# Pooled attention and MLP mixer on one core: u transposed in pairs, a second v buffer, and the fourth batch's loads in another order

## The chip, the core and the metric

The kernel runs on one core of a Trainium2 chip. The metric is the device time of one execution in microseconds; lower is better. Before the change it is 290.57 us, the median of 3 runs from 289.85 to 290.57.

## What is computed

Eight batches, each with q, k, v of 8 heads x 576 positions x 64. Keys and values are averaged over groups of 8 positions (576 become 72), softmax attention runs over the 72, and the result x (576 x 512 per batch) goes through a token-mixing and a channel-mixing MLP, each with its residual:

```
k_p, v_p = mean over groups of 8 positions of k, v          # 72 x 64 per head
x  = softmax(q k_p^T / 8) v_p                               # heads side by side: 576 x 512
u  = x + (relu(x^T w_tok1) w_tok2)^T                        # 576 -> 256 -> 576 along positions
out = u + relu(u w_ch1) w_ch2                               # 512 -> 1536 -> 512 along channels
```

Inputs and output are float32; the kernel computes in bfloat16 and sums in float32.

## The kernel before

A batch's 576 positions are cut into 4 chunks of 128 (main) and a tail of 64; the tails of two batches share one tile of 128 (pairs 0 and 7, 1 and 2, 3 and 4, 5 and 6). Below, "second batch" is `b` = 1, "fourth batch" is `b` = 3, and so on.

One batch passes these steps. Loads by GpSimd's queue, which cast to bfloat16 on the way (`load`: k into `km`, q into `qm`, v into `vs`, tails into `kt` and `qt`). q transposed by DMA on SyncE's queue (`qT_dma`, L540; for the first two batches by TensorE). k pooled by matmuls (`pool_k`); v pooled by matmuls for the first two batches (`pool_v`, L288) and by adds on GpSimd for the others (`sum_v`, L298 to L300). Scores of two units of half the main positions each (`a` and `c` in the code; the first and the second unit) and a tail unit (`do_S`, L326, with the row maximum and the subtraction on VectorE, L329 and L331), the exponential on ScalarE (`do_E`, L339), the probabilities transposed by DMA from SyncE's queue (`do_PT`, L346, two for a unit; for the first two batches by TensorE), and their product with v (`do_AV`, L387). Token mixing (`do_AT`, L472; `do_u`, L510, its sum with x on VectorE, L515). Then u is transposed (`do_uT`, L526: by DMA for all but the first batch, one transfer for each chunk of 128 positions into `uTm`, laid out as 4 blocks of channels x 512 positions). Channel mixing reads it (`channel_mix`): L756 multiplies `w_ch1` with a whole row of 512 positions, so it needs all four chunks; ScalarE applies the ReLU into `GT` (L758); L771 multiplies `GT` with `w_ch2`, chunk by chunk, VectorE adds u (L775), and the output goes out by SyncE's queue (L803).

The order of work is written out. `weave` mixes two lists of steps by their estimated costs: the channel mixing of batch b as the main list, and beside it the value products and token mixing of batch b + 1 and the scores of batch b + 2. Every engine takes its instructions strictly in that order, and so does each queue: SyncE issues transposes and outputs one after the other, and GpSimd both issues the loads and does the sums of v. A step of cost 0 is put in without moving the others.

The loads of the first four batches are issued ahead, as far as buffers allow; those of batch b + 2 from the fifth on wait for a gate: GpSimd copies one column of the second unit's last transposed probabilities (L739) and then issues the loads.

```
def load_gated(b, ready):
    nc.gpsimd.tensor_copy(out=gate, in_=ready())
    load(b, (0, 2, 1) if slot_of[b] else (0, 1, 2))      # 0 is k, 1 is q, 2 is v
    sum_v(b)
```

k and q have two buffers, v has one, so that the fourth batch's v is loaded after the third's is summed, from the list of the second batch (L670, L671). `GT` has two buffers. PSUM gives six buffers to all the matmuls' results. At most eight loads of GpSimd's queue are in flight: the next one waits for the landing of the one eight before it; the same holds for SyncE's queue.

Of the kernel before, what the change touches and what calls it, by code (L numbers as in the profile page):

```python
# [9 lines left out]
BF16 = mybir.dt.bfloat16  # L10
# [5 lines left out]
class Stream:  # L16
# [5 lines left out]
    def add(self, cost, fn):  # L22
        self.items.append((cost, fn))
# [25 lines left out]
def kernel(  # L49
# [16 lines left out]
    nc = tc.nc  # L66
# [15 lines left out]

    singles = ctx.enter_context(tc.tile_pool(name="singles", bufs=1))
    kv_pool = ctx.enter_context(tc.tile_pool(name="kv", bufs=2))
    v_pool = ctx.enter_context(tc.tile_pool(name="vp", bufs=1))
    sum_pool = ctx.enter_context(tc.tile_pool(name="sums", bufs=1))
    tail_pool = ctx.enter_context(tc.tile_pool(name="tl", bufs=2))
    pt_pool = ctx.enter_context(tc.tile_pool(name="ptp", bufs=6))
# [4 lines left out]
    u_pool = ctx.enter_context(tc.tile_pool(name="up", bufs=2))  # L93
    at_pool = ctx.enter_context(tc.tile_pool(name="atp", bufs=3))
    ut_pool = ctx.enter_context(tc.tile_pool(name="utail", bufs=2))
    gt_pool = ctx.enter_context(tc.tile_pool(name="gt", bufs=2))
    out_pool = ctx.enter_context(tc.tile_pool(name="outp", bufs=4))
    ps = ctx.enter_context(tc.tile_pool(name="ps", bufs=6, space=bass.MemoryType.PSUM))
    ps_tr = ctx.enter_context(tc.tile_pool(name="ps_tr", bufs=2, space=bass.MemoryType.PSUM))
# [15 lines left out]

    def load(b, which=(0, 1, 2)):
        g = group_of[b]
        if (b == 2 or g > 1 and slot_of[b] == 0) and 0 in which:
            tail_t[b] = [tail_pool.tile([P, H, D], BF16, name=n) for n in ("kt", "qt")]
            if b == 2:  # L120
                for t in tail_t[b]:
                    nc.gpsimd.memset(t[half[0]], 0.0)
            else:
                tail_t[groups[g][1]] = tail_t[b]
        main_t.setdefault(b, [None] * 3)
        for i in which:
            src = (k, q, v)[i]
            if i == 2 and b > 1:

                vs = v_pool.tile([P, H, POOL, D], BF16, name="vs")  # L130
                nc.gpsimd.dma_start(out=vs[0:SP].rearrange("p h t d -> p h (t d)"),
                                    in_=src[b].rearrange("h (p t) d -> p h (t d)", t=POOL))
                main_t[b][i] = vs
                continue
            mt = (v_pool.tile([P, H, POOL, D], BF16, name="vs")[:, :, 0:NJ, :] if i == 2 else
                  kv_pool.tile([P, H, NJ, D], BF16, name=("km", "qm")[i]))
            main_t[b][i], tt = mt, tail_t[b][i]
            nc.gpsimd.dma_start(out=mt.rearrange("p h j d -> p h (j d)"),
                                in_=src[b, :, 0:MAIN, :].rearrange("h (p j) d -> p h (j d)", j=NJ))

            for bb in [b] if g < 2 else groups[g] if slot_of[b] == 0 else []:
                nc.gpsimd.dma_start(out=tt[half[slot_of[bb]]], in_=src[bb, :, MAIN:S, :].rearrange("h p d -> p h d"))
# [316 lines left out]
    def token_mix(b):  # L459

        g, s = group_of[b], slot_of[b]
        ATs[b] = singles.tile([P, 2, DM], BF16, name="AT0") if b == 0 else at_pool.tile([P, 2, DM], BF16, name="AT")

        def acts(m, at_ps):
            if m == 0:
                nc.scalar.activation(out=ATs[b][:, m, :], in_=at_ps, func=AF.Relu)  # L466
            else:
                nc.vector.tensor_scalar(out=ATs[b][:, m, :], in0=at_ps, scalar1=0.0, scalar2=None, op0=ALU.max)  # L468

        def mains(m, at_ps):  # L470
            for j in range(NJ):
                nc.tensor.matmul(out=at_ps, lhsT=w1m[:, j, m * P:(m + 1) * P], rhs=x_main[b][:, j, :],  # L472
                                 start=(j == 0), stop=False)

        def tails(m, at_ps):
            nc.tensor.matmul(out=at_ps, lhsT=w1t[s][:, m * P:(m + 1) * P], rhs=x_tail[g], start=False, stop=True)  # L476

        def do_AT(m):
            at_ps = ps.tile([P, DM], FP32, name="pa")
            mains(m, at_ps)  # L480
            tails(m, at_ps)
            acts(m, at_ps)

        at_both = []

        def do_both_AT(js, tail, last):

            fresh = not at_both
            if fresh:
                at_both.extend(ps.tile([P, DM], FP32, name="pa") for _ in range(2))  # L490
            for i, j in enumerate(js):
                for m in range(2):
                    nc.tensor.matmul(out=at_both[m], lhsT=w1m[:, j, m * P:(m + 1) * P], rhs=x_main[b][:, j, :],
                                     start=(fresh and i == 0), stop=(last and i == len(js) - 1))
            if tail:
                for m in range(2):
                    nc.tensor.matmul(out=at_both[m], lhsT=w1t[s][:, m * P:(m + 1) * P], rhs=x_tail[g],
                                     start=False, stop=False)
            if last:
                for m in range(2):  # L500
                    acts(m, at_both[m])

        def do_u(j):
            u_ps = ps.tile([P, DM], FP32, name="pa")
            by_act = b == 0 and j % 2 == 1
            if j < NJ:
                if by_act:
                    nc.tensor.matmul(out=u_ps, lhsT=ident, rhs=x_main[b][:, j, :], start=True, stop=False)
                for m in range(2):
                    nc.tensor.matmul(out=u_ps, lhsT=w2m[:, m, j, :], rhs=ATs[b][:, m, :],  # L510
                                     start=(m == 0 and not by_act), stop=(m == 1))
                if by_act:
                    nc.scalar.copy(out=u_main[b][:, j, :], in_=u_ps)
                else:
                    nc.vector.tensor_tensor(out=u_main[b][:, j, :], in0=u_ps, in1=x_main[b][:, j, :], op=ALU.add)  # L515
            else:
                for i in range(4):
                    nc.tensor.matmul(out=u_ps, lhsT=w2t[i // 2][:, i % 2, :], rhs=ATs[groups[g][i // 2]][:, i % 2, :],  # L518
                                     start=(i == 0), stop=(i == 3))
                nc.vector.tensor_tensor(out=u_tail[g], in0=u_ps, in1=x_tail[g], op=ALU.add)  # L520

        def do_uT(j):
            us = u_main[b][:, j, :] if j < NJ else u_tail[g]
            if b > 0:
                dst = uT_main[b][:, :, j * P:(j + 1) * P] if j < NJ else uT_tail[g]
                nc.sync.dma_start_transpose(out=dst, in_=us)  # L526
                return
            uT_ps = ps_tr.tile([P, 4, P], BF16, name="pt")
            for kk in range(4):
                nc.tensor.transpose(out=uT_ps[:, kk, :], in_=us[:, kk * P:(kk + 1) * P], identity=ident)  # L530
            copy = nc.scalar.copy if j % 2 else nc.vector.tensor_copy
            copy(out=uT_main[b][:, :, j * P:(j + 1) * P], in_=uT_ps)

        return do_AT, do_both_AT, do_u, do_uT

# [31 lines left out]
    def mix_stream(st, b, pooled=()):  # L567
# [1 line left out]
        g, s = group_of[b], slot_of[b]  # L569
        add = adder(st)  # L570
        u_main[b] = u_pool.tile([P, NJ, DM], BF16, name="um")
        uT_main[b] = u_pool.tile([P, 4, MAIN], BF16, name="uTm")
        if s == 1:
            u_tail[g] = ut_pool.tile([P, DM], BF16, name="ut")
            uT_tail[g] = ut_pool.tile([P, 4, P], BF16, name="uTt")
# [4 lines left out]
        add(1080, do_AT, 1)  # L580
        for bb in pooled:
            add(KP, pool_k, bb)
        nj = NJ + s
        for j in range(nj + 1):
            if j < nj:
                add(690, do_u, j)
            if j >= 1:
                add(0 if b else 224, do_uT, j - 1)

    def first_stream():  # L590

# [53 lines left out]
    def second_stream(st):  # L645
# [21 lines left out]
        add(AV, a.do_AV, 0)  # L667
        add(SC, c.do_S, 2)
        add(0, t.do_E)
        add(0, load, 3, (2,))  # L670
        add(0, sum_v, 3)  # L671
        add(AV, a.do_AV, 1)
        add(0, c.do_E, 2)
        add(PT, t.do_PT)
# [62 lines left out]
    def load_gated(b, ready):  # L737

        nc.gpsimd.tensor_copy(out=gate, in_=ready())  # L739
        load(b, (0, 2, 1) if slot_of[b] else (0, 1, 2))  # L740
        sum_v(b)

    def channel_mix(uTs, us, dst, width, early=0):
# [6 lines left out]
        def do_GT(m0):  # L750
            def f():
                g_ps = ps.tile([P, per, width], FP32, name="pa")
                for i in range(per):
                    m = m0 + i
                    for kk in range(4):
                        nc.tensor.matmul(out=g_ps[:, i, :], lhsT=wc1[:, kk, m * P:(m + 1) * P], rhs=uTs[:, kk, :],  # L756
                                         start=(kk == 0), stop=(kk == 3))
                nc.scalar.activation(out=GT[:, m0:m0 + per, :], in_=g_ps, func=AF.Relu)  # L758
            return f
# [22 lines left out]
        def do_early(m, hold, t0, t1):  # L782
            def f():
                if t0 == 0:
                    hold[m] = ps.tile([P, width], FP32, name="pa")
                for kk in range(4):
                    nc.tensor.matmul(out=hold[m][:, t0:t1], lhsT=wc1[:, kk, m * P:(m + 1) * P], rhs=uTs[:, kk, t0:t1],
                                     start=(kk == 0), stop=(kk == 3))
                if t1 == width:
                    nc.scalar.activation(out=GT[:, m, :], in_=hold[m], func=AF.Relu)  # L790
# [6 lines left out]
    def c_stream(b):  # L797
# [8 lines left out]
            for s, bb in enumerate(groups[g]):  # L806
                nc.sync.dma_start(out=out[bb, MAIN:S, :], in_=o_sb[half[s], :])

        wide, chunk = channel_mix(uT_main[b], lambda j: u_main[b][:, j, :], dst_main, MAIN, 0 if b else 3)
        blocks = [wide] + [chunk(j, 2 if b == B - 1 and j == NJ - 1 else 1) for j in range(NJ)]  # L810
        if slot_of[b] == 1:
            wide, chunk = channel_mix(uT_tail[g], lambda j: u_tail[g], dst_tail, P)
            at = 3 if b == B - 1 else len(blocks)
            blocks[at:at] = [wide, chunk(0)]
        for block in blocks:
# [7 lines left out]
    load(1)  # L823
    load_w_ch2()
    load(2)
    load(3, (0, 1))
    sum_v(2)
    engines = {mybir.EngineType.PE, mybir.EngineType.Activation, mybir.EngineType.DVE,
               mybir.EngineType.SP, mybir.EngineType.Pool}
# [42 lines left out]
```

## Time and profile before

| | |
|---|---|
| median of 3 runs | 290.57 us (289.85 to 290.57) |
| profiled execution, first to last instruction (span) | 288.5 us |
| TensorE busy | 271.0 us (94%) |
| VectorE / ScalarE / GpSimd busy | 162.4 / 121.3 / 101.5 us |
| mean granted TensorE clock | 0.994 |
| moved by DMA | 42.68 MB, 148 GB/s |

A run's time has about 2 us beside the span. In the profile PE is TensorE's matmul, PEld its weight load, DVE VectorE, ACT ScalarE, POOL GpSimd and SP SyncE; a q behind a name is the engine's sequencer, which waits and issues DMAs. A row of a timeline gives the start, the duration, the engine, the line, the operation, the tiles (out<-in), shapes, the number of instructions merged, and in brackets how long the engine had been idle and what ended that. Rows for a tile or line give the shortest, median and longest duration in ns, and the time from a DMA's issue to its landing. Consecutive rows of PE overlap by some 0.2 us, since matmuls are pipelined.

### The profile page before, as it was taken

The page shows a single profiled execution, that of the slowest core. Times are in us where ns is not written, and L with a number is a line of the kernel's source. Part 1 is how long each engine was busy: PE and PEld are TensorE (multiplying, and loading weights), DVE is VectorE, ACT ScalarE, POOL GpSimd, SP SyncE. Part 2 cuts the span into 40 slices and gives each one's busy share as a digit, 9 for nine tenths or more (in the row PEclk, how much of TensorE's full clock was granted, in tenths as well). Part 3 has the DMA queues.
Part 4 walks back from the last instruction along what each step waited for, and adds up shares of the span by engine and source line. Part 5 has one row for each costly group of instructions (what it writes and reads, how often), then busy time and mean ns, then how long its engine had stood idle before and what let it go on. Part 6 is the DMA issues. An engine that isn't in the chain of part 4 may idle for free.

```text
span 288.5 us, 5632 instructions
## 1 busy us (share of the span) xinstructions
PE 271.0 (94%) x2210; PEld 147.1 (51%) x2246; DVE 162.4 (56%) x371; ACT 121.3 (42%) x222; POOL 101.5 (35%) x147
## 2 busy tenths in 40 slices
PE   6888998885999999999999999999999999999995
PEld 4554755442445554446545554465445444464463
DVE  4676268687356985386647953684558642530012
ACT  8572887113442355114553365035442561026320
POOL 8666634292780836129508423570000000000000
PEclk9999999999899999999999999999999999999999
DMA  7999999999959999998999799959524820241013
GB/s 84 185 205 198 196 204 192 174 203 146 252 88 169 166 214 195 182 183 166 172 185 155 170 218 153 157 165 162 115 54 97 194 58 36 93 109 39 27 45 110
DMA packets 102714, 42.68 MB, mean 148 GB/s; under 512 B 72480, under 2 KB 98080, under 8 KB 102688
## 3 DMA queue, kind: packets, MB, share of 16 engines
q0 software_dynamic: 36688, 17.93, 47.2%
q1 hardware_dynamic: 65856, 24.26, 43.7%
q8 instruction: 17, 0.28, 0.4%
q10 hardware_dynamic: 144, 0.13, 0.1%
q14 instruction: 9, 0.07, 0.1%
HBM read 35.85 MB, written 9.44 MB: 157 GB/s over the span
## 4 chain that ended last, share of the span: by engine, by line
PE 82%; DMA 7%; DVE 6%; ACT 3%; issue 1%; DVEq 0%
PE pa L756 31%; PE pa L771 28%; DMA qT<-qm 4%; PE pa L510 4%; PE pa L472 4%; PE pa L387 3%; DMA uTm<-um 3%; PE pa L253 2%; PE pa L326 2%; DVE sh L331 2%; DVE mx L329 1%; PE pa L267 1%; ACT prob_m L339 1%; PE pa L518 1%; ACT pT L352 1%
## 5 line engine op out<-in xcount | busy, mean ns | idle before, releaser
L771 PE MATMUL pa<-wc,GT 128*128 128x512 bf16 (+1 forms) x429 | 102.7, 373 | 1.0 <-DVE sh L331 0.2
L756 PE MATMUL pa<-uTm,wc 128*128 128x512 bf16 x357 | 90.1, 384 | 3.8 <-DMA uTm<-um 3.1
L758 ACT ACTIVATE GT<-pa 128x512 bf16<-128x512 f32 x105 | 62.5, 597 | 66.5 <-PE pa L756 62.4
L756 PEld LDWEIGHTS <-wc 128*128 128x128 bf16 x564 | 45.4, 98 | 40.6 <-DVE o L775 3.6
L771 PEld LDWEIGHTS <-GT 128*128 128x128 bf16 x444 | 41.5, 98 | 40.4
L339 ACT ACTIVATE prob_m<-sh 128x432 bf16<-128x432 f32 (+1 forms) x48 | 24.7, 522 | 60.9 <-DVE sh L331 51.1
L298 POOL TENSOR_TENSOR s<-vs 72x512 f32<-72x512 bf16 x24 | 27.6, 1148 | 49.7 <-DMA vs<-in_v_dram 48.2
L775 DVE TENSOR_TENSOR o<-pa,um 128x512 f32<-128x512 f32 (+1 forms) x33 | 22.1, 670 | 25.3 <-PE pa L771 25.3
L329 DVE TENSOR_REDUCE mx<-pa 128x6 f32<-128x432 f32 (+1 forms) x48 | 26.4, 550 | 7.6 <-PE pa L326 7.5
L331 DVE TENSOR_TENSOR sh<-pa,mx 128x432 f32<-128x432 f32 (+1 forms) x48 | 26.8, 558 | 5.1 <-DVE mx L329 0.5
L391 DVE RECIPROCAL den<-pa 128x4 f32<-128x4 f32 (+1 forms) x66 | 11.6, 176 | 24.5 <-PE pa L387 24.4
L515 DVE TENSOR_TENSOR um<-pa,xm 128x512 bf16<-128x512 f32 x30 | 20.2, 687 | 8.6 <-PE pa L510 8.6
L392 DVE TENSOR_TENSOR xm<-pa,den 128x256 bf16<-128x256 f32 x56 | 23.8, 424 | 1.9
L510 PE MATMUL pa<-AT,w2m 128*128 128x512 bf16 x64 | 18.3, 379 | 0.5 <-ACT AT L466 0.5
L299 POOL TENSOR_TENSOR s<-s 72x256 f32<-72x256 f32 x24 | 17.3, 722 | 1.9
L468 DVE TENSOR_SCALAR AT<-pa 128x512 bf16<-128x512 f32 x8 | 5.5, 692 | 21.8 <-PE pa L476 21.1
L387 PEld LDWEIGHTS <-pT 72*128 72x128 bf16 (+1 forms) x280 | 12.4, 100 | 8.8 <-issue 1.7
L326 PE MATMUL pa<-kbd,qT 128*128 128x144 bf16 x128 | 15.5, 226 | 1.4 <-DMA qT<-qm 0.9
L326 PEld LDWEIGHTS <-qT 128*128 128x128 bf16 x128 | 10.7, 98 | 10.5 <-DMA qT<-qm 1.4
L387 PE MATMUL pa<-vpx,pT 72*128 72x65 bf16 (+1 forms) x280 | 14.1, 194 | 1.1 <-DVE pT L352 0.5
L472 PE MATMUL pa<-xm,w1m 128*128 128x512 bf16 x54 | 14.4, 379 | 0.4 <-DVE xm L392 0.2
L253 PE MATMUL pa<-idle 128*128 128x288 bf16 (+2 forms) x40 | 9.8, 379 | 2.3 <-DVE pool_t L178 2.2
(122 smaller groups left out, 232.8 us busy)
## 6 DMA issues: line engine op xcount, KB each, us to landing
out_dram<-o SPq DMA_DIRECT2D x31, 256.0 KB, 2.6
km<-in_k_dram POOLq DMA_DIRECT2D x8, 512.0 KB, 7.7
qm<-in_q_dram POOLq DMA_DIRECT2D x7, 512.0 KB, 12.7
vs<-in_v_dram POOLq DMA_DIRECT2D x6, 576.0 KB, 10.1
wc<-in_moe_w_ch_dram POOLq DMA_DIRECT2D x6, 512.0 KB, 12.4
out_dram<-o SPq DMA_DIRECT2D x9, 128.0 KB, 2.4
vs<-in_v_dram POOLq DMA_DIRECT2D x2, 512.0 KB, 9.9
kt<-in_k_dram POOLq DMA_DIRECT2D x8, 64.0 KB, 7.7
```

The costliest lines, as they stand in the source:

```text
L298: nc.gpsimd.tensor_tensor(out=s4, in0=vs[:, hs, 0:4], in1=vs[:, hs, 4:8], op=add)
L326: nc.tensor.matmul(out=sc[:, (h - h0) * 2:(h - h0) * 2 + 2, :], lhsT=qTs[self.b][:, 2 * h + self.jj, :], rhs=kbd[self.b % NB][:, h], start ...
L329: nc.vector.tensor_reduce(out=mx[:, 0:n], in_=sc, axis=AX.X, op=ALU.max)
L331: nc.vector.tensor_tensor(out=sh[:, 0:n], in0=sc, in1=mx[:, 0:n, None].broadcast_to([P, n, SP]), op=ALU.subtract)
L339: nc.scalar.activation(out=self.probs[:, :, h0:h1, 0:SP].rearrange("p e h n -> p h e n"), in_=self.sh[i][:, 0:(h1 - h0) * 2].rearrange("p ...
L387: nc.tensor.matmul(out=ao[r, hh, :], lhsT=probs_of(h, r), rhs=vpx[b % NB][:, h, :], start=True, stop=True)
L392: nc.vector.tensor_tensor(out=xo[rows, hf * HP * D:(hf + 1) * HP * D].rearrange("p (h d) -> p h d", d=D), in0=ao[rows, :, 0:D], in1=den[ro ...
L472: nc.tensor.matmul(out=at_ps, lhsT=w1m[:, j, m * P:(m + 1) * P], rhs=x_main[b][:, j, :], start=(j == 0), stop=False)
L510: nc.tensor.matmul(out=u_ps, lhsT=w2m[:, m, j, :], rhs=ATs[b][:, m, :], start=(m == 0 and not by_act), stop=(m == 1))
L756: nc.tensor.matmul(out=g_ps[:, i, :], lhsT=wc1[:, kk, m * P:(m + 1) * P], rhs=uTs[:, kk, :], start=(kk == 0), stop=(kk == 3))
L758: nc.scalar.activation(out=GT[:, m0:m0 + per, :], in_=g_ps, func=AF.Relu)
L771: nc.tensor.matmul(out=hold["ps"], lhsT=GT[:, kk, j * P:(j + 1) * P], rhs=wc2[:, kk, cols], start=(kk == 0), stop=(kk == NM - 1))
```

## The change

Five edits. u is transposed by one DMA for two chunks, issued after the second of the two (`do_uT(j, 2)` after j = 1 and j = 3), and the tail's by one of its own as before; `uTm` is laid out as chunk x channel block x position for that, so that L756's operand of 512 positions becomes four runs of 128. `GT` has one buffer. v has two. The fourth batch's q is loaded ahead of its k. Its v is no longer loaded and summed in the second batch's list but behind the fifth batch's gate: v of the fourth, the fifth's loads, then both sums.

```diff
-    v_pool = ctx.enter_context(tc.tile_pool(name="vp", bufs=1))
+    v_pool = ctx.enter_context(tc.tile_pool(name="vp", bufs=2))
...
-    gt_pool = ctx.enter_context(tc.tile_pool(name="gt", bufs=2))
+    gt_pool = ctx.enter_context(tc.tile_pool(name="gt", bufs=1))
...
-        if (b == 2 or g > 1 and slot_of[b] == 0) and 0 in which:
+        if (b == 2 or g > 1 and slot_of[b] == 0) and b not in main_t:
...
-        def do_uT(j):
-            us = u_main[b][:, j, :] if j < NJ else u_tail[g]
+        def do_uT(j, n=1):
             if b > 0:
-                dst = uT_main[b][:, :, j * P:(j + 1) * P] if j < NJ else uT_tail[g]
+                us = u_main[b][:, j:j + n].rearrange("p j d -> p (j d)") if j < NJ else u_tail[g]
+                dst = uT_main[b][:, j:j + n].rearrange("p j k n -> p (j k) n") if j < NJ else uT_tail[g]
                 nc.sync.dma_start_transpose(out=dst, in_=us)
                 return
+            us = u_main[b][:, j, :]
...
-            copy(out=uT_main[b][:, :, j * P:(j + 1) * P], in_=uT_ps)
+            copy(out=uT_main[b][:, j], in_=uT_ps)
...
-        uT_main[b] = u_pool.tile([P, 4, MAIN], BF16, name="uTm")
+        uT_main[b] = u_pool.tile([P, NJ, 4, P], BF16, name="uTm")
...
-        nj = NJ + s
-        for j in range(nj + 1):
-            if j < nj:
-                add(690, do_u, j)
-            if j >= 1:
-                add(0 if b else 224, do_uT, j - 1)
+        for j in range(NJ + s):
+            add(690, do_u, j)
+            if j in (1, 3):
+                add(0, do_uT, j - 1, 2)
+        if s:
+            add(0, do_uT, NJ)
...
-        add(0, load, 3, (2,))
-        add(0, sum_v, 3)
...
         nc.gpsimd.tensor_copy(out=gate, in_=ready())
+        if b == 4:
+            load(3, (2,))
         load(b, (0, 2, 1) if slot_of[b] else (0, 1, 2))
+        if b == 4:
+            sum_v(3)
         sum_v(b)
...
-        ... rhs=uTs[:, kk, :],
+        ... rhs=uTs(kk, 0, width),
...
-        wide, chunk = channel_mix(uT_main[b], lambda j: u_main[b][:, j, :], dst_main, MAIN, 0 if b else 3)
+        wide, chunk = channel_mix(lambda kk, t0, t1: uT_main[b][:, t0 // P:t1 // P, kk, :],
+                                  lambda j: u_main[b][:, j, :], dst_main, MAIN, 0 if b else 3)
...
-    load(3, (0, 1))
+    load(3, (1, 0))
```

More of the change, by code (lines that the diff above doesn't have):

```diff
@@ L755, in f @@
                     for kk in range(4):
-                        nc.tensor.matmul(out=g_ps[:, i, :], lhsT=wc1[:, kk, m * P:(m + 1) * P], rhs=uTs[:, kk, :],
+                        nc.tensor.matmul(out=g_ps[:, i, :], lhsT=wc1[:, kk, m * P:(m + 1) * P], rhs=uTs(kk, 0, width),
                                          start=(kk == 0), stop=(kk == 3))
@@ L786, in f @@
                 for kk in range(4):
-                    nc.tensor.matmul(out=hold[m][:, t0:t1], lhsT=wc1[:, kk, m * P:(m + 1) * P], rhs=uTs[:, kk, t0:t1],
+                    nc.tensor.matmul(out=hold[m][:, t0:t1], lhsT=wc1[:, kk, m * P:(m + 1) * P], rhs=uTs(kk, t0, t1),
                                      start=(kk == 0), stop=(kk == 3))
@@ L807, in dst_tail @@
                 nc.sync.dma_start(out=out[bb, MAIN:S, :], in_=o_sb[half[s], :])
-        wide, chunk = channel_mix(uT_main[b], lambda j: u_main[b][:, j, :], dst_main, MAIN, 0 if b else 3)
+        wide, chunk = channel_mix(lambda kk, t0, t1: uT_main[b][:, t0 // P:t1 // P, kk, :],
+                                  lambda j: u_main[b][:, j, :], dst_main, MAIN, 0 if b else 3)
         blocks = [wide] + [chunk(j, 2 if b == B - 1 and j == NJ - 1 else 1) for j in range(NJ)]
         if slot_of[b] == 1:
-            wide, chunk = channel_mix(uT_tail[g], lambda j: u_tail[g], dst_tail, P)
+            wide, chunk = channel_mix(lambda kk, t0, t1: uT_tail[g][:, kk, t0:t1], lambda j: u_tail[g], dst_tail, P)
             at = 3 if b == B - 1 else len(blocks)
```

## The prediction

> **What bounds the kernel now.** I read first the page's head, then the table by windows, then the timelines of PE, SP and POOL around the one stretch that stands out, then the landing times of the transfers used there.
>
> ```profile
> span 288.5 us, 5632 instructions
> PE 271.0 (94%) x2210; PEld 147.1 (51%) x2246; DVE 162.4 (56%) x371; ACT 121.3 (42%) x222; POOL 101.5 (35%) x147
> ```
>
> TensorE is busy for 271.0 of 288.5 us, so only PE's idle time, or matmuls that run slowly, can be won. The change alters no matmul: listed engine by engine, the two programs have the same instructions in the same order on PE, DVE and ACT. Only the queues of POOL and SP differ. The median of the runs, 290.57, lies 2.1 us above the profiled span; that part lies around the span, and I carry differences of the span over to the median one to one.
>
> In the windows, columns are the stretch, its length, busy time of PE, PEld, DVE, ACT, POOL, the granted clock, DMA share and GB/s:
>
> ```profile
> 70.00:75.00 5.00, 3.51 (x9) 1.30 (x10) 1.01 (x2) 1.13 (x3) 1.78 (x2) 0.66 1.15 213
> 68.35:71.49 3.14, 0.01 (x2) 0.03 (x1) 2.45 (x5) 1.52 (x3) 0.00 (x0) 0.99 1.24 149
> 71.40:74.82 3.42, 3.33 (x8) 1.20 (x9) 0.00 (x0) 0.60 (x1) 1.60 (x2) 0.50 1.21 240
> ```
>
> After the opening (the first 30 us) this is the one stretch with a hole: PE stands for 3.14 us, and then runs for 3.42 us at a granted clock of 0.50. The timeline of PE says what ended the hole:
>
> ```profile
> 61.65 0.36 PE L326 MATMUL pa<-kbd,qT 128*128 128x144 bf16 x3 [0.94 <-DMA qT<-qm]
> 66.46 1.89 PE L771 MATMUL pa<-wc,GT 128*128 128x512 bf16 x8
> 71.49 5.24 PE L756 MATMUL pa<-uTm,wc 128*128 128x512 bf16 x16 [3.13 <-DMA uTm<-um]
> ```
>
> The second batch's channel mixing (L756) waits for its transposed u, and its first matmuls are the slow ones. So the hole costs 3.13 us of waiting and half of 3.42 us, 1.71, of lost clock: 4.84 us.
>
> **The pairs, at the hole.** These are SP's queue and POOL's queue there:
>
> ```profile
> 59.31 1.20 SPq L526 DMA_TRANSPOSE uTm<-um  x1
> 61.10 0.33 SPq L803 DMA_DIRECT2D out_dram<-o  x1
> 61.48 3.83 SPq L526 DMA_TRANSPOSE uTm<-um  x3
> 66.02 5.25 SPq L346 DMA_TRANSPOSE pT<-prob_m  x2
> 65.06 0.86 POOL L131 DMA_DIRECT2D vs<-in_v_dram  x1
> 73.14 1.15 POOL L298 TENSOR_TENSOR s<-vs 72x512 f32<-72x512 bf16 x1 [6.73 <-DMA vs<-in_v_dram]
> ```
>
> The last of the four transposes is issued at 61.48 + 3.83 - 1.27 = 64.04 (its row is below) only because SP takes about 1.25 us for each. When are its data ready? DVE's rows:
>
> ```profile
> 58.59 1.89 DVE L515 TENSOR_TENSOR um<-pa,xm 128x512 bf16<-128x512 f32 x3 [0.44 <-PE pa L510]
> 60.99 0.68 DVE L515 TENSOR_TENSOR um<-pa,xm 128x512 bf16<-128x512 f32 x1
> 62.04 0.61 DVE L329 TENSOR_REDUCE mx<-pa 128x6 f32<-128x432 f32 x1 [0.37 <-PE pa L326]
> ```
>
> Chunk 3 of u is written at 61.67. With pairs SP issues chunks 0 and 1 at about 59.9 (chunk 1 is the second of the three in 58.59 to 60.48), the output, and chunks 2 and 3 at 61.7. The last issue comes 64.04 - 61.7 = 2.3 us earlier, and 28 issues become 14. What a pair takes to land is shown by the probabilities' transposes, which are 8 blocks of 128 columns as a pair is, against the 4 blocks of a single chunk:
>
> ```profile
> L526 SPq DMA_TRANSPOSE uTm<-um x1: 1273/1273/1273, 64.0 to 64.0; - x1
> DMA to landing us min/median/max: 7.3/7.3/7.3
> L526 SPq DMA_TRANSPOSE uTm<-um x4: 1190/1211/1225, 211.9 to 215.8; - x4
> DMA to landing us min/median/max: 2.4/2.4/2.5
> L346 SPq DMA_TRANSPOSE pT<-prob_m x2: 1247/1335/1423, 73.7 to 75.1; - x2
> DMA to landing us min/median/max: 3.3/3.3/3.4
> ```
>
> Alone, a chunk lands in 2.4 us and 8 blocks in 3.3. The 7.3 at the hole is contention with the fourth batch's v, issued at 65.06 and landed at 73.1. That load is moved away, which matters as much as the pairing. So the last pair lands between 61.7 + 3.3 = 65.0 (no contention) and 61.7 + 7.3 = 69.0 (as slow as now). Up to about 64.4 the opening's loads are still beside it; the last of them is this piece of the fourth batch's q, whose place a piece of k takes:
>
> ```profile
> L142 POOL DMA_DIRECT2D qt<-in_q_dram x1: 677/677/677, 49.3 to 49.3; - x1
> DMA to landing us min/median/max: 15.1/15.1/15.1
> ```
>
> So contention covers part of the pair's time and none of the rest; I take 67.5, a little above the middle. PE has finished the work before it at 66.46 + 1.89 = 68.35. The wait goes, and with it the slow clock: **-4.84**.
>
> The Trainium skill, "TensorE: Matmul & The Clock Gate", part 1, puts the drop to half clock after an idle window of about 3.4 us, counted in a free-running window. Here 3.13 us were enough, and the slow stretch lasted 3.42; the 0.94 us before it drew none. By the page any remainder of the wait would leave the clock alone; by the row a remainder near 3 us would not.
>
> **What is late next.** With the hole gone PE wants the second unit's probabilities 4.84 earlier. ACT's last exponential there, the first and the last of its value products now, POOL's gate and first load behind it, and the fourth batch's first value product:
>
> ```profile
> 70.45 0.44 ACT L339 ACTIVATE prob_m<-sh 128x288 bf16<-128x288 f32 x1 [0.36 <-DVE sh L331]
> 76.57 0.42 PE L387 MATMUL pa<-vpx,pT 72*128 72x65 bf16 x8
> 81.29 0.42 PE L387 MATMUL pa<-vpx,pT 72*128 72x65 bf16 x8
> 83.24 0.19 POOL L739 COPY gate<-pT 128x1 bf16<-128x1 bf16 x1
> 83.36 0.92 POOL L138 DMA_DIRECT2D km<-in_k_dram  x1
> 105.18 0.42 PE L387 MATMUL pa<-vpx,pT 72*128 72x65 bf16 x8
> ```
>
> The first unit's pT goes out from 66.02 on, 1.3 us each, and the second of its two lands by 67.3 + 3.3 = 70.6; its use starts at 76.57 - 4.84 = 71.7. The second unit's can go at 70.9 and 72.3 and land at 74.2 and 75.6; the last is wanted at 81.29 - 4.84 = 76.4: met by 0.8 us. ACT is busy until 70.89 with the exponential before its first ReLU of this batch, while PE's first group would be done near 69.2. The six PSUM buffers take up such a lag, or it costs up to its 1.7 us; since the value products between the groups give ACT time, I take +0.2.
>
> **The moved v and sums.** POOL is free from about 66 then, so the gate is passed when the second unit's pT lands, at 75.6 instead of 83.24. Behind it now stand four loads: the fourth batch's v, then k, v, q of the fifth. A v issued at 65.06 took until 73.1, 8 us; from 75.8 it lands by about 84, and the sums (from 73.14 to the gate at 83.24, 10.1 us) end at 94. The fourth batch's value products, at 105.18 - 4.84 = 100.3, want them: 6 us of cover. The fifth's sums then run until 104.5, wanted a whole batch later. Cost 0; without that cover each us of lateness costs one.
>
> **Reordered first loads.** With the second v buffer the third batch's v goes out before the fourth's loads, and that batch's q before k; the number in flight and the bytes are the same. The q transpose that PE awaited at 61.65 meets v's long packets for less of its time. Bounds: -0.94 (the wait goes) to +1 (it grows as much); DVE cannot start its scores before 61.67 instead of 62.04, so I take -0.3. The fourth's k is now last, at about 64.4, wanted after 80: nothing.
>
> **Layout and GT.** The moving operand of L756 is now four runs of 128 columns. The only rows with a moving operand in pieces are the v pooling of batches 0 and 1 (eight runs of 64):
>
> ```profile
> L288 PE MATMUL pa<-vs,pool_m x8: 377/379/379, 13.9 to 37.4; 128*72 128x512 bf16 x8
> L756 PE MATMUL pa<-uTm,wc x357: 377/379/634, 33.3 to 269.0; 128*128 128x512 bf16 x179
> ```
>
> Both 379 ns: 0. The single GT buffer makes ACT's first ReLU of a batch wait for the last L771 that reads the old one; PE runs that before the L756 which the ReLU awaits anyway: 0, and no cover to lose.
>
> **Sum.** -4.84 + 0.2 - 0.3 = -4.9. From 290.57: **285.7** (span 283.6).
>
> **The rivals.** A: the pair lands late after all. For it: the loads end at 64.4 as before, and an output stands between the pairs. Against: no load after that. At the upper bound, 69.0, and with an output's 1 us, a wait of 0.7 to 1.7 us stays and the gain is 3.2 to 4.2: 286.4 to 287.4; with the clock drop kept as well, 289.1.
>
> B: a new hole at the third batch's u, where four loads stand now instead of three.
>
> ```profile
> 89.35 4.23 SPq L526 DMA_TRANSPOSE uTm<-um  x3
> 94.48 1.35 SPq L526 DMA_TRANSPOSE uTm<-um  x1
> DMA to landing us min/median/max: 6.7/6.7/6.7
> ...
> L138 POOL DMA_DIRECT2D qm<-in_q_dram x1: 905/905/905, 85.1 to 85.1; - x1
> DMA to landing us min/median/max: 12.7/12.7/12.7
> 103.46 1.89 PE L756 MATMUL pa<-uTm,wc 128*128 128x512 bf16 x8
> ```
>
> The last chunk lands at 94.48 + 6.7 = 101.2, 3.4 after the last load (85.1 + 12.7 = 97.8), 2.3 before PE wants it. The three loads took 14.4 us from their issue at 83.36, at most 4.8 each. With the gate at 75.6 and 4.8 for the v more, they end by 95, and u lands between then (both pairs go out before the output, no longer behind it) and 98.4; wanted at 98.6. If the loads start 2 us later than I think, up to 2 us are lost: 287.7.
>
> C, the slower side: the fourth batch's v comes too late. It decides from a landing at 90 on. PE then stands at 100.3, and a hole over about 3 us also draws the half clock, 1.71. To end slower than before by what a run can tell, v must land after 94, 18 us after its issue: 291.5. Only loads issued into the saturated opening took near that (15.1, above), and from 64.4 to 75.6 no load is in flight, so little speaks for it.
>
> **How the numbers follow.** Forecast 0.72, A 0.13, B 0.09, C 0.06. The range reaches down by the bound on the first q transpose (-4.84 - 0.94 with ACT's term at 0, or 284.8, and 0.2 for the scatter of the runs: 284.6) and up through A's and B's likely part: 284.6 to 288.0. A measurement of this kernel can tell about 0.3%, 0.87 us. Faster by more: all of the forecast, most of A and B: 0.90. Within: the rest of A and B, and some of C, 0.04. Slower: C, 0.06.
>
> **What would show it.** In the profile after: no idle over 0.5 us ahead of the second batch's L756 and a clock of 1.00 between 65 and 80; 14 transposes of u; gate near 75.6, fourth batch's sums ended near 94, no DMA wait at 100; L756 still at 379 ns. Wrong if the hole moves to the third batch's u (B) or the value products wait for POOL (C), or if the transposes of u still take 7 us with no load beside them.

## The result, and the profile after

| | before | after |
|---|---|---|
| median of 4 runs each, same chip | 290.57 us (289.85 to 291.85) | 286.73 us (286.16 to 286.83) |
| ratio of the times | | 0.9859, 95% interval 0.9833 to 0.9886 |
| profiled execution, span | 288.5 us | 284.9 us |

The change is faster by 3.84 us, 1.4%. The forecast was 285.7, the range 284.6 to 288.0.

The head of the page of the changed kernel, with its row of the granted clock in 40 slices, and one row of the table by windows (stretch, length, busy time of PE, PEld, DVE, ACT, POOL, clock, DMA share, GB/s):

```profile
span 284.9 us, 5640 instructions
PE 271.6 (95%) x2246; PEld 146.3 (51%) x2246; DVE 162.5 (57%) x371; ACT 121.3 (43%) x222; POOL 101.8 (36%) x147
PEclk9999999999999999999999999999999999999999
65.00:80.00 15.00, 14.14 (x104) 7.04 (x102) 10.76 (x31) 8.15 (x15) 3.67 (x5) 1.00 1.10 206
```

PE's work is the same (2,246 weight loads in both pages; the page before lacks the records of 36 matmuls); what went is idle time and slow clock. The stretch that held the hole is now at full clock. PE's timeline (lines of the changed kernel: L759 is the former L756, L774 the former L771):

```profile
61.32 0.36 PE L326 MATMUL pa<-kbd,qT 128*128 128x144 bf16 x3 [0.48 <-DMA qT<-qm]
66.14 1.89 PE L774 MATMUL pa<-wc,GT 128*128 128x512 bf16 x8
68.89 3.61 PE L759 MATMUL pa<-uTm,wc 128*128 128x512 bf16 x16 [0.86 <-DMA uTm<-um]
72.34 0.42 PE L387 MATMUL pa<-vpx,pT 72*128 72x65 bf16 x8
101.28 0.43 PE L387 MATMUL pa<-vpx,pT 72*128 72x65 bf16 x8 [0.17 <-DMA pT<-prob_m]
105.36 0.45 PE L387 MATMUL pa<-vpx,pT 72*64 72x65 bf16 x16
```

At u the wait is 0.86 us instead of 3.13. The first value products after it start 4.23 us earlier than before (72.34 against 76.57), those of the fourth batch 3.90 earlier (101.28 against 105.18). From there on PE keeps that lead: VectorE's last sum of an output starts at 281.17 instead of 285.05. The span is shorter by 3.6 only, because the last output lands 0.3 later after its issue.

The second pair of u, by SP's queue (rows of the tile), and POOL's queue after the gate:

```profile
L526 SPq DMA_TRANSPOSE uTm<-um x1: 2883/2883/2883, 61.9 to 61.9; - x1
DMA to landing us min/median/max: 6.8/6.8/6.8
```

```profile
75.59 0.19 POOL L738 COPY gate<-pT 128x1 bf16<-128x1 bf16 x1 [12.28 <-DMA pT<-prob_m]
76.15 0.88 POOL L131 DMA_DIRECT2D vs<-in_v_dram  x1 [0.36 <-PE pa L759]
84.00 1.15 POOL L298 TENSOR_TENSOR s<-vs 72x512 f32<-72x512 bf16 x1 [4.37 <-DMA vs<-in_v_dram]
103.97 0.45 POOL L300 TENSOR_TENSOR vpx<-s 72x128 bf16<-72x128 f32 x1
```

The pair is issued at 61.95 and lands at 68.75. Its issue holds SyncE for 2.88 us, until 64.83; the first pair's took 1.24. The moved v lands at 83.9, its sums end at 94.2 and the fifth batch's at 104.4.

### The profile page after: what moved, and what is told of

It is laid out like the page before. It is cut to its first block, busy times and chain, and to the rows that moved or that the text cites. A ratio compares the mean times of both kernels' runs of the same rounds, so it can differ in the third digit from the quotient of the medians.

```text
span 284.9 us, 5640 instructions
## 1 busy us (share of the span) xinstructions
PE 271.6 (95%) x2246; PEld 146.3 (51%) x2246; DVE 162.5 (57%) x371; ACT 121.3 (43%) x222; POOL 101.8 (36%) x147
## 4 chain that ended last, share of the span: by engine, by line
PE 80%; DVE 7%; DMA 6%; ACT 3%; POOL 1%; issue 1%; DVEq 0%; POOLq 0%
PE pa L759 31%; PE pa L774 28%; PE pa L510 4%; PE pa L472 4%; PE pa L387 3%; DMA uTm<-um 2%; DMA pT<-prob_m 2%; DMA qm<-in_q_dram 2%; PE pa L326 2%; DVE sh L331 2%; DVE mx L329 1%; PE pa L267 1%; PE pa L518 1%; DVE um L515 1%; PE pa L476 1%; ACT prob_m L339 1%
## 5 line engine op out<-in xcount | busy, mean ns | idle before, releaser
L774 PE MATMUL pa<-wc,GT 128*128 128x512 bf16 (+1 forms) x444 | 104.1, 373 | 0.0
L759 PE MATMUL pa<-uTm,wc 128*128 128x512 bf16 x372 | 89.8, 379 | 0.9 <-DMA uTm<-um 0.9
L759 PEld LDWEIGHTS <-wc 128*128 128x128 bf16 x564 | 45.0, 98 | 37.1 <-DVE mx L329 1.3
L774 PEld LDWEIGHTS <-GT 128*128 128x128 bf16 x444 | 41.5, 98 | 40.4
## 6 DMA issues: line engine op xcount, KB each, us to landing
vs<-in_v_dram POOLq DMA_DIRECT2D x2, 512.0 KB, 10.2
```

The source lines that it names most:

```text
L774: nc.tensor.matmul(out=hold["ps"], lhsT=GT[:, kk, j * P:(j + 1) * P], rhs=wc2[:, kk, cols], start=(kk == 0), stop=(kk == NM - 1))
```

## The experiments

The theory (called V in most of the expectations): the fourth batch's v, loaded beside the transposes of u and of the probabilities, made the hole, and moving it is the gain. Its rivals are the pairing, the order of q and k, the single GT buffer, and, for what is left, the outputs in SyncE's queue. Each ratio is against the kernel before on the same chip. Edits move line numbers: L756, L757 and L759 below are the same multiplication with `w_ch1`.

**u chunk by chunk.** The changed kernel with the old four transposes.

```diff
-            if j in (1, 3):
-                add(0, do_uT, j - 1, 2)
...
+            if j >= 1:
+                add(0, do_uT, j - 1)
```

> The changed kernel with u transposed chunk by chunk again (same new layout, one DMA per chunk, in the old order); all else as changed. Theory V (the hole came from the fourth batch's v load beside u's transposes): with that load away the last single chunk, issued near 64, still lands near 68 to 69, the wait ahead of the second batch's L759 is 1.2 us or less, no half clock, 286.5 to 287.5 us. Theory P (the hole came from SP's four issues): the last chunk is late by the 2.3 us of later issue, the wait is 2 to 3 us and may draw the half clock, 288 to 290 us.

Measured: 287.15 us (286.91 to 287.88), ratio 0.9878 [0.9850, 0.9906]; span 285.5. PE's timeline of this kernel:

```profile
69.40 3.61 PE L759 MATMUL pa<-uTm,wc 128*128 128x512 bf16 x16 [1.23 <-DVE sh L331]
```

The last chunk is issued at 63.96, 2.0 us later than the pair, and lands 5.3 us after that, near 69.3: 0.5 later than the pair and 0.1 before the row starts. So that landing, not the named VectorE, is most likely what came last. Most of what pairs save in issuing is lost again in landing (6.8 us against 5.3). Nearly the whole gain is there without pairs; what pairing adds, 0.4 us by the medians and 0.6 by the ratios, lies inside the two intervals.

**v back in the second batch's list.** The changed kernel with the fourth batch's v loaded and summed where it was; having two buffers, v is now issued at 54.0, earlier than in the kernel before.

```diff
+        add(0, load, 3, (2,))
+        add(0, sum_v, 3)
...
-        if b == 4:
-            load(3, (2,))
...
-        if b == 4:
-            sum_v(3)
```

> The changed kernel with the fourth batch's v load and sums put back into the second batch's list (v keeps two buffers, so that the load can go out as soon as GpSimd comes to it, near 54 us, and stands behind the k of that batch in the loads' queue). Theory V: v's packets run beside the last pair of u, which lands at 71 or later, wait 3 us and more with the half clock, 289.5 to 291 us. Theory P: the pairs are issued early all the same, wait about 1 us, 286.5 to 287.5 us.

Measured: 292.59 us (291.32 to 294.07), ratio 1.0060 [1.0036, 1.0085]: slower than before the change. The rows of u's tile, PE's timeline and the table by windows:

```profile
L526 SPq DMA_TRANSPOSE uTm<-um x2: 1321/3074/4826, 61.9 to 63.9; - x2
DMA to landing us min/median/max: 10.8/11.1/11.4
```

```profile
74.80 5.23 PE L757 MATMUL pa<-uTm,wc 128*128 128x512 bf16 x16 [4.40 <-DMA uTm<-um]
```

```profile
74.70:78.11 3.41, 3.31 (x8) 1.20 (x9) 0.00 (x0) 0.60 (x1) 3.10 (x5) 0.50 0.92 214
```

With that load beside them (it lands at 71.3) the pairs take 10.8 and 11.4 us instead of 6.0 and 6.8, and hole and half clock are back, larger: 4.40 + 1.71 = 6.1 us against 4.84 before. The 1.3 us between the two lie inside what the ratio shows (1.0 to 2.5 us). The profiled execution (294.02 us) is one of the longer ones: in its opening, before the moved load is issued, two waits and a half-clock stretch had already made PE 1.9 us later (L449 at 49.40 against 47.53 in the changed kernel).

**The pairs and the layout alone, in the kernel before.**

```diff
-                dst = uT_main[b][:, :, j * P:(j + 1) * P] if j < NJ else uT_tail[g]
+                us = u_main[b][:, j:j + n].rearrange("p j d -> p (j d)") if j < NJ else u_tail[g]
+                dst = uT_main[b][:, j:j + n].rearrange("p j k n -> p (j k) n") if j < NJ else uT_tail[g]
...
+            if j in (1, 3):
+                add(0, do_uT, j - 1, 2)
```

> The kernel before with the pairs and their layout alone (one v buffer, two of GT, the old order of loads, v of the fourth batch issued near 65). Theory P: wait about 1 us, no half clock, 286.5 to 287.5 us. Theory V: the pair is issued 2.3 us earlier but v's packets from about 67.6 on catch its end and the probabilities' transposes after it: a wait of 1 to 3 us at L757 and new waits of 1 to 2 us at the value products, 288 to 290.5 us.

Measured: 291.22 us (289.70 to 292.41), ratio 1.0012 [0.9988, 1.0037]: nothing, and above what either theory expected. PE's timeline and the rows of the probabilities' tile:

```profile
69.25 3.61 PE L757 MATMUL pa<-uTm,wc 128*128 128x512 bf16 x16 [0.76 <-DMA uTm<-um]
75.63 0.43 PE L387 MATMUL pa<-vpx,pT 72*128 72x65 bf16 x8 [2.76 <-DMA pT<-prob_m]
```

```profile
L346 SPq DMA_TRANSPOSE pT<-prob_m x3: 1777/2077/3267, 66.2 to 72.8; - x3
L445 SPq DMA_TRANSPOSE pT<-prob_t x1: 1857/1857/1857, 70.8 to 70.8; - x1
DMA to landing us min/median/max: 5.9/7.8/9.4
```

The pairs do what they were forecast to do at u: the wait falls to 0.76, less than theory V expected. But v, issued at 66.3, then runs beside the probabilities instead; the first of them takes 9.4 us, PE waits 2.76 for it, and the clock is halved from 76.7 to 80.1 (theory V expected waits of 1 to 2 us there). The hole has only moved by one step of the queue.

**k ahead of q.** The changed kernel with the first loads of the fourth batch in the old order.

```diff
-    load(3, (1, 0))
+    load(3, (0, 1))
```

> The changed kernel with the fourth batch's k loaded ahead of its q again, all else as changed. Both theories: the same bytes stand in the queue until about 65, so the q transpose of the third batch and the pair of u land within 0.5 us of the changed kernel's 61.3 and 68.8; the fourth batch's q transpose, issued near 74, does not wait; 286.3 to 287.2 us. If the order of q and k was what helped, the time goes up by over 1 us.

Measured: 286.70 us (285.95 to 288.17), ratio 0.9868 [0.9823, 0.9913]. The pair lands at 68.5, the wait at u is 0.87. The order does nothing.

**One GT buffer, in the kernel before.**

```diff
-    gt_pool = ctx.enter_context(tc.tile_pool(name="gt", bufs=2))
+    gt_pool = ctx.enter_context(tc.tile_pool(name="gt", bufs=1))
```

> The kernel before with one GT buffer and nothing else. My step: the wait is covered by PE's own order, so within 0.3% of the kernel before, and the same 3 us hole at 68 us. If one buffer costs, each batch's first ReLU would start later and PE would idle at each batch's first L756, 1 us or more in all.

Measured: 290.86 us against 291.04, ratio 0.9981 [0.9954, 1.0009]: nothing. PE's timeline in this profile shows the loss of the kernel before in another form:

```profile
61.93 0.36 PE L326 MATMUL pa<-kbd,qT 128*128 128x144 bf16 x3 [1.50 <-DMA qT<-qm]
70.02 3.61 PE L756 MATMUL pa<-uTm,wc 128*128 128x512 bf16 x16 [1.39 <-DMA uTm<-um]
75.08 0.43 PE L387 MATMUL pa<-vpx,pT 72*128 72x65 bf16 x8 [1.45 <-DMA pT<-prob_m]
103.07 1.89 PE L756 MATMUL pa<-uTm,wc 128*128 128x512 bf16 x8 [0.93 <-DVE sh L331]
105.87 0.43 PE L387 MATMUL pa<-vpx,pT 72*128 72x65 bf16 x8 [0.92 <-DMA pT<-prob_m]
```

The expected 3 us hole isn't there. Five waits of 0.92 to 1.50 us at full clock, 6.19 in all, stand where the profile before has 0.94 and 3.13 of waiting and 1.71 of clock, 5.78 in all; the spans are 289.1 and 288.5.

One GT buffer need not be the reason, for the kernel before does the same. Of its 70 executions timed beside these experiments, 27 have a mean granted clock of 0.998 or more; a stretch of 3.41 us at half clock would take 0.006 off the mean, so these hold no whole one. Chip by chip their medians are 290.9 to 291.1 us, and those of the 38 executions between 0.99 and 0.998 are 290.2 to 291.2. So the form of the loss varies from execution to execution, and its price hardly does.

**The load left out.** The kernel before without the load of the fourth batch's v: the sums read the third batch's instead. All else, the four single chunks too, is as before.

```diff
+            if i == 2 and b == 3:
+                main_t[b][i] = main_t[2][2]
+                continue
```

> The kernel before with the fourth batch's v load left out (its sums read the third batch's v again), all else as before: four single transposes, two GT buffers. This prices the load alone. Theory V: with nothing beside them the transposes of u and of the third batch's probabilities land by 69 and 71, the wait ahead of L756 is 1.2 us or less and draws no half clock: 286.3 to 287.3 us, the whole gain of the change. If the load's place is only part of it: 288 to 290 us.

Measured: 286.43 us (285.99 to 286.89), ratio 0.9851 [0.9818, 0.9884], the same as the change's. PE's timeline here, and the rows of the queues between 66 and 73 us (packets, MB, share of the 16 engines; q1 is SyncE's queue with the transposes and outputs, q0 GpSimd's with the loads), first of the kernel before, then of this one:

```profile
69.13 3.61 PE L759 MATMUL pa<-uTm,wc 128*128 128x512 bf16 x16 [0.55 <-DVE mx L332]
```

```profile
q1 hardware_dynamic: 2033, 0.50, 59.0%
q0 software_dynamic: 784, 0.59, 54.1%
```

```profile
q1 hardware_dynamic: 4410, 1.31, 87.2%
```

Taking that one load away is worth the whole gain. In these seven of the eight microseconds in which it ran, SyncE's queue moved 0.50 MB; without it, 1.31 MB. The Trainium skill, "DMA: Bandwidth & Descriptors", section "Queues, rings and completion order", says that each DMA engine serves the queues that have work in turn, a packet at a time. The two sums, 0.59 and 0.50 MB, don't contradict such a sharing, but no run here shows the turns: the rows count 784 and 2,033 packets, and whether these are the page's packets isn't shown. A single transfer beside the load takes about three times as long (7.3 us against 2.4 for a chunk of u, 9.4 against 3.3 for probabilities); that figure the page doesn't give.

**The fourth batch's k later, and the outputs later.** Two attempts at the 0.86 us left: k issued only when the first unit's probabilities have landed (near 70), so that the opening's loads end earlier; and the first batch's two outputs issued behind u's pairs.

```diff
+        if b == 2:
+            add(0, load_k3, lambda: a.pT[1][:, 0, 0:1])
...
-    load(3, (1, 0))
+    load(3, (1,))
```

> The changed kernel with the fourth batch's k taken out of the opening's loads and issued when the first unit's probabilities of the third batch have landed (near 71). If what is left of the wait for u is contention with the loads that run until 65, the last pair lands near 66 instead of 68.8, the 0.9 us wait goes, the q transpose lands up to 1 us earlier, k lands near 79, before its use near 82: 285.3 to 286.2 us. If what is left is the order in SP's queue (outputs ahead of u's pairs), the pair still lands near 68.5 and the time stays at 286.5 to 287; if the late k meets the second unit's probabilities, a new wait of 1 us at the value products.

```diff
+                while b == 1 and j == 2 and held:
+                    held.pop(0)()
...
+            held.append(send) if b == 0 and j < 2 else send()
```

> The changed kernel with the first two outputs of the first batch issued behind the second pair of u instead of ahead of the pairs. Queue order theory: the last pair lands 1 us earlier or more, the 0.9 us wait goes, 285.7 to 286.3 us. Load theory: the pair lands within 0.3 us of 68.8, 286.4 to 287 us.

Measured: k late 291.95 us, ratio 1.0034 [1.0010, 1.0058]; outputs late 286.97 us, ratio 0.9867 [0.9829, 0.9906]. With k late, the rows of k's tile, of the second pair of u, PE's timeline and the windows:

```profile
L138 POOL DMA_DIRECT2D km<-in_k_dram x1: 920/920/920, 70.3 to 70.3; - x1
DMA to landing us min/median/max: 7.3/7.3/7.3
L526 SPq DMA_TRANSPOSE uTm<-um x1: 1951/1951/1951, 61.9 to 61.9; - x1
DMA to landing us min/median/max: 4.2/4.2/4.2
```

```profile
77.20 0.62 PE L387 MATMUL pa<-vpx,pT 72*128 72x65 bf16 x8 [2.64 <-DMA pT<-prob_m]
80.01 0.62 PE L387 MATMUL pa<-vpx,pT 72*128 72x65 bf16 x8 [0.48 <-DMA pT<-prob_m]
```

```profile
76.66:83.48 6.82, 5.58 (x27) 2.43 (x29) 2.24 (x8) 1.19 (x2) 3.00 (x5) 0.50 1.26 202
```

The wait at u is gone (the pair, with no load beside it, takes 4.2 us and lands at 66.1), but k now runs from 70.3 to 77.7 beside the second unit's probabilities. They take 6.6 and 8.1 us, and 2.64 us of waiting brings 6.8 us of half clock besides. With the outputs late the pair takes 5.8 us, lands at 67.3, and the wait at u is gone too. PE's timeline says where it went:

```profile
64.06 0.32 PE L424 MATMUL pa<-kbd,qTt 64*64 64x72 bf16 x8 [0.47 <-DMA qTt<-qt]
101.52 0.43 PE L387 MATMUL pa<-vpx,pT 72*128 72x65 bf16 x8 [1.01 <-DMA pT<-prob_m]
```

PE comes earlier to the fourth batch's value products, whose probabilities stand beside the gated loads until 95.8.

**Both together.** The two edits above in one kernel.

> Both edits, k late and the two outputs behind the pairs. Either theory: the pair lands at 66 or earlier, no wait ahead of the second batch's L759; what is then left is the q transpose and the start of the fourth batch's value products: 285.0 to 286.0 us. If it is not below the better of the two single edits, the wait is no longer what bounds this stretch.

Measured: 292.20 us, ratio 1.0045 [1.0019, 1.0071], with k's hole (2.77 us at 77.3) unchanged. The last pair, with neither the load beside it nor an output ahead of it:

```profile
L528 SPq DMA_TRANSPOSE uTm<-um x1: 1279/1279/1279, 61.8 to 61.8; - x1
DMA to landing us min/median/max: 3.1/3.1/3.1
```

The four kernels together split the pair's 6.8 us: without the load it takes 4.2, without the outputs 5.8, without either 3.1.

**The fifth batch's v behind the next gate.** The changed kernel with three loads instead of four behind the fifth batch's gate; and the same with the outputs late.

```diff
-        if b == 4:
-            load(3, (2,))
-        load(b, (0, 2, 1) if slot_of[b] else (0, 1, 2))
+        if b in (4, 5):
+            load(b - 1, (2,))
+        load(b, (0, 1) if b == 4 else (0, 2, 1) if slot_of[b] else (0, 1, 2))
```

> The changed kernel with one more v moved: the fifth batch's v (and its sums) goes behind the sixth batch's gate, so that the fifth's gate starts three loads again (v of the fourth, k and q of the fifth). If the 0.2 to 0.3 us ahead of the fourth batch's first value product at 101 (its probabilities' transposes land late behind four loads) comes from the length of that burst, the loads end near 92 instead of 95.4, that wait goes, and the time is 0.2 to 0.4 us below the changed kernel's: 286.2 to 286.6 us. If four loads behind the sixth's gate are late for the fourth or fifth batch there, PE waits near 128 to 135 and the time is 287.5 us or more.

> Both that move and the two outputs of the first batch behind the pairs. With the outputs alone the wait for u went, but 1.0 us came back at 101; if that came from the burst, both together keep the gain: 285.4 to 286.3 us. If it stays at 286.7 to 287, the wait at 101 has another cause.

Measured: 307.88 us, ratio 1.0612 [1.0562, 1.0663]; and 307.86 us, ratio 1.0588 [1.0554, 1.0622]. Of the first, the row of the waits (total, times, longest) and PE's timeline:

```profile
PE pa L387 <- POOL vpx L300: 18.1, 4, 11.4
```

```profile
116.11 0.32 PE L387 MATMUL pa<-vpx,pT 72*64 72x65 bf16 x4 [11.44 <-POOL vpx L300]
```

The waiting matmuls are those of the tail tile (72*64), which the fourth and the fifth batch share: it needs the fifth's v a batch sooner than its main positions do. In the changed kernel these matmuls start at 105.36 and the last sum of the fifth's v ends at 104.42 (rows above): the cover is 0.9 us, not a batch.

**The fifth batch's q last.** The first of these kernels taught that v can't move; q of the fifth batch, which lands last of the four, is first used at 121.4. Here it is loaded behind both sums, with the outputs late.

```diff
-        load(b, (0, 2, 1) if slot_of[b] else (0, 1, 2))
+        load(b, (0, 2) if b == 4 else (0, 2, 1) if slot_of[b] else (0, 1, 2))
...
+        if b == 4:
+            load(b, (1,))
```

> The changed kernel with the first batch's two outputs issued behind u's pairs, and the fifth batch's q, the last of the four loads behind the gate, issued only after both sums of v, near 104.5 us instead of 78.7. In the changed kernel q landed at 95.4 and the fourth batch's first probabilities, issued at 95.4, took 5.9 us; with the outputs moved the wait at u was gone and PE waited 1.0 us for those probabilities. Theory V (a load beside a DMA transpose is what makes the transpose late): the gated loads end near 91.5, the third batch's pairs of u land by 92, the probabilities take 3.3 us, PE waits for neither, and the span falls from 284.9 to between 283.7 and 284.3: a time of 285.6 to 286.2. The transposed q of the fifth batch, wanted at 120.2, lands between 112 and 121, since it now stands beside the sixth batch's loads; each us beyond 120 costs one. Rival H (what stands in front of those probabilities in SyncE's queue sets their landing, not the loads): they still take 5 us or more, the wait of 1.0 us stays, and the time is 287. Rival L (the late q only moves the hole): a wait of 2 us or more ahead of the fifth batch's scores, with the half clock: 288 to 291.

Measured: 296.07 us (294.32 to 297.08), ratio 1.0143 [1.0097, 1.0189]; span 294.3. The fourth batch's first probabilities, in the changed kernel and in this one:

```profile
L346 SPq DMA_TRANSPOSE pT<-prob_m x1: 1897/1897/1897, 95.4 to 95.4; - x1
DMA to landing us min/median/max: 5.9/5.9/5.9
```

```profile
L346 SPq DMA_TRANSPOSE pT<-prob_m x1: 1280/1280/1280, 94.7 to 94.7; - x1
DMA to landing us min/median/max: 3.3/3.3/3.3
```

So the transpose does what theory V forecast: without q's load it takes 3.3 us, and the wait of 0.17 to 1.01 us at 101 is gone. In the changed kernel that load ended just as the transpose was issued, so it was not beside it; it stood beside the pairs of u ahead of the transpose, which took 9.6 and 8.3 us there and 7.6 and 6.2 here. That the pairs passed the delay on is argued, not shown by itself. Against rival H: the same transfers stand ahead of the transpose in SyncE's queue in both. But rival L happened, with a wait six times as long as the one that went and a time above the 288 to 291 expected of it. PE's timeline, the rows of q's transpose and the windows of this kernel:

```profile
105.44 0.23 PE L387 MATMUL pa<-vpx,pT 72*64 72x65 bf16 x3 [0.70 <-POOL vpx L300]
127.88 0.54 PE L326 MATMUL pa<-kbd,qT 128*128 128x144 bf16 x3 [6.47 <-DMA qT<-qm]
```

```profile
L545 SPq DMA_TRANSPOSE qT<-qm x1: 5761/5761/5761, 111.7 to 111.7; - x1
DMA to landing us min/median/max: 16.2/16.2/16.2
```

```profile
127.80:134.70 6.90, 6.82 (x24) 3.07 (x25) 3.66 (x7) 1.12 (x2) 6.13 (x8) 0.57 0.43 125
```

q's transpose now stands beside the sixth batch's loads and takes 16.2 us; it was expected by 121 and lands at 127.8. PE waits 6.47 us and then loses 0.43 of 6.90 us, 2.97, to the clock. And the sums' cover of 0.9 us, with PE a microsecond ahead, turns into a wait of 0.70.

No kernel tried is faster than the changed one by what can be told.

## Why the prediction was right, and where it was off

- **The hole at u, -4.84.** Right in kind: waiting and half clock were one loss, and the clock stays at 1.00. Off in size: -3.98 (3.13 - 0.86, and the 1.71 of clock). The mis-sized term is the landing of the last pair: forecast 67.5, between 65.0 and 69.0; measured 68.75, 6.8 us after its issue, where a pair late in the kernel takes 3.0. The forecast let the contention end with the opening's loads. These ended at 64.9, about as forecast (64.4), and the pair landed 3.9 us later. Of the 3.7 us that the pair took above the 3.1 it needs with neither load nor outputs in its way, the load is worth 2.6 (4.2 without it). The other 1.1 are the outputs' share, which the forecast put at nothing and only rival A counted, as 1 us. This is rival A at its lower end: 0.86 us of wait stays, over the 0.5 that the prediction set as its sign, and 286.73 lies in A's 286.4 to 287.4. It was A, given 0.13, that came true, and not the forecast's own course, given 0.72; the number is near because what A leaves of the wait is short and drew no half clock.
- **The form of the loss.** 3.13 of waiting and 1.71 of clock are the profiled execution's. In 27 of 70 executions of the kernel before there was no half-clock stretch, at the same time. That one profile gave the price of the usual loss was luck in part.
- **What carries it.** The prediction said that moving v matters as much as the pairing. The runs say more: v's load is the whole loss (left out: 0.9851; changed kernel: 0.9859), pairs without its move are worth nothing (1.0012), pairs on top 0.4 to 0.6 us, not told from nothing.
- **ACT's lag, +0.2.** 0 measured: PE runs from the first L759 to the value products at 72.34 as fast as it can, 16 matmuls in 3.61 us.
- **q's transposes, -0.3.** -0.33 measured (61.32 against 61.65). In four profiles with the old first loads the row starts between 61.65 and 61.93, in seven with the new ones (either order of q and k) between 60.91 and 61.48. The order of q and k is not its cause: put back, it left the start at 61.01. What else in the changed loads does it was not separated.
- **The moved v and sums, 0.** Gate 75.59 (75.6 forecast), v landed 83.9 (84), sums ended 94.2 (94) and 104.4 (104.5). Where the step failed is "wanted a whole batch later": the shared tail wants the fifth's sums at 105.4, 0.9 us after their end. The cost was still 0, with far less cover than told. The prediction's rival C looked for this danger at the fourth's v and not at the fifth's.
- **The third batch's u (rival B).** The loads ended at 95.4 (95 forecast), the pairs at 95.3 and 96.4, and L759 started at 99.2 without a wait. What had not been foreseen is the next transfer behind them: the fourth batch's probabilities took 5.9 us, and 0.33 us of the lead are lost there (4.23 to 3.90).
- **Layout and GT, 0.** L759 over all its matmuls on main positions stands in the page of the changed kernel with the mean of the forecast, and GT alone is at 0.9981 [0.9954, 1.0009].

```profile
L759 PE MATMUL pa<-uTm,wc 128*128 128x512 bf16 x372 | 89.8, 379 | 0.9 <-DMA uTm<-um 0.9
```

In sum: -3.98 - 0.33 + 0.33 + 0.3 (the last output's landing) = -3.7, against -3.6 by the spans and -3.84 by the medians.

## What to carry to other kernels

A load whose data nobody wants yet can still be the longest wait of a kernel, if it runs beside small transfers that someone does want: list what stands in the other queue during its flight before choosing its place. Shortening the transfer that PE waited for only moved the hole to the next one in that queue, and in the profiles every load put beside transposes with little cover (issued at 54, 66, 70 and 105 us) brought a hole of 2.6 to 6.5 us (with one GT buffer the same loss came as five shorter waits). Before a producer is called early, find its first reader in the timeline; here a tile shared by two batches read it a batch sooner than the loop suggests.

## What the runs showed of the hardware

The half clock followed holes shorter than one stretch of it. In the profiled executions, after the opening, waits of 2.76, 3.13 and 4.40 us were each followed by one stretch of 3.41 us at a granted clock of 0.50. The waits of 2.64 and 2.77 us with k late had one of 6.8 us, which began 0.5 us before they ended; the wait of 6.47 us had one of 10.2, from 123.5 to 133.7. Single waits of up to 1.50 us drew none after the opening, but in the opening of the profile with v back in the list two waits of 1.36 and 1.09 us, at 13 and 15.6 us, were followed by a stretch of 3.4. So the length of a single wait does not decide it alone.

The Trainium skill, "TensorE: Matmul & The Clock Gate", part 1, has a free-running window of 3.4 us and the drop after an idle one: the stretches of 3.41 us agree with that length, and with it a hole of 2.64 us can't have filled a window, so that a window needn't be wholly idle. A wait near 3 us cost in these profiles half its length to more than its length again in clock: 1.71 for 3.13, and up to 3.41 for 2.64, where a second slow window followed.

A DMA transpose beside a load on the other queue took 5.9 to 16.2 us in the rows above, against 2.4 to 3.3 where no load and no other transfer held it up. Issuing the last transpose of u 2.0 us earlier in such company, as a pair instead of a chunk, brought the landing forward by 0.5.
